# Whole-array matmuls issued as four column tiles, whole key tiles for VectorE, and later kernel loads in a gated attention and convolution kernel

## The chip, the cores and the metric

The kernel runs on one core of a Trainium2 chip. The metric is the device time of one execution in microseconds (us). The core has five engines that run side by side and each in program order: TensorE (PE; its weight loads are listed as PEld), VectorE (DVE), ScalarE (ACT), GpSimd (POOL) and SyncE (SP, which here only issues DMAs).

## The reference

The input x has 2048 tokens of 640 features. Two branches are mixed by a gate g = sigmoid(x . gate_w):

```
k_shift = causal 4-tap convolution of A_k by A_shift_k, per feature;  kv = k_shift * A_v
a = x * (causal long convolution of kv by A_ssm_k over 2048 tokens, by FFT + kv * A_ssm_D)
q = x @ wq (32 heads of 20);  k = x @ wk;  v = x @ wv   (one key and value head for all)
b = softmax(q k^T / sqrt(20)) v, heads joined, @ wo
out = g * a + (1 - g) * b
```

## The kernel before, in words

**Work.** The attention scores are 32 groups G, each of four heads and 512 queries (8 groups for each of four query blocks). A group has 16 key tiles j of 128 keys. So there are 32 x 16 x 4 = 2048 score tiles (G, j, r) of 128 keys by 512 queries, r being the head within the group. A head has 20 features, with a bound on the score in row 20, so the score matmul (`score`, L1462) uses a 32-row strip of the array, at row 32 r, and four heads can run side by side. The product with the values (`PVmm`, L1542) uses a 32-column strip, four heads side by side again, and adds up over the 16 key tiles in PSUM bank 6.

**Who takes the exponential.** Most tiles go to ACT. They are cut into units of alternately three and two tiles (`stream`); PSUM banks 0 to 2 hold a three-tile unit and banks 3 and 4 a two-tile one. ACT writes their exponentials to ETA (1536 elements per partition) or ETB (1024), L1499. The other tiles go to DVE, without an exponential: for each (G, j) listed in `DVE_J`, two of the four heads are left out of the units; DVE turns each score tile into 16-bit integers (L1526, PSUM to the scratch PS in ES), and then makes four versions of it with four shifts (`dexp`, L1535), each 1024 elements because it covers both heads. Four products with differently weighted values (vneg) add up to the exponential. `DEXP` holds all of this. Groups 0, 1 and 31 have no DVE tiles.

**The rest.** The convolutions are matmuls too: L1802 (four taps as diagonal matrices), L1883 to L1893 (the spectra of kv and of the long kernel, with tables of cosines in TE and TO), the product of spectra on POOL (L1912), and L1937 (back to time). Query projections (L1353) and output projections (L1970, L1675, at the end L1705) complete them. These use the whole 128 by 128 array, and their results leave PSUM banks 5 and 7 (for projections of the output 6 as well) through DVE. The score tiles for DVE use banks 5 and 7 also.

**Order.** A scheduler in the kernel (`Scheduler`) walks through modelled time and writes a fixed order for each engine. PE's main queue has the score units and the value products; in the gaps before the next unit's bank comes free it places other work (`pick_work`), and dummy matmuls on a zero tile (L2031, the filler) when PE's busy share over a window falls below `FILL`. A charge `SWITCH` stands for a change between the row-strip, column-strip and whole-array forms; the forms are named by `MODE`. The order of the first 400 operations is set by a table of priorities `PRO`.

**Loads.** Query rows of block 0 reach the tile qT0 by way of DRAM: the projections are stored to scr_q, read back (`q_ld`, qT<-scr_q), and four further DMAs bring the row with the bound (`crow`, qT<-cr). The long kernel is loaded in five parts by transposing DMAs (kst<-in_A_ssm_k_dram, L1815, in `ssm_rows`) and stored to scr_k (scr_k<-kst). All of these are issued by SP.

Of the kernel before, what the change touches and what calls it, by code (L numbers as in the profile page):

```python
# [25 lines left out]
SLA = 0.5  # L26
SLB = 0.5
SLACK = 0.05
SLACK0 = 0.8
FILL = 0.7  # L30
# [3 lines left out]
MODE = {"qk": "r", "dqk": "r", "pv": "c", "fillc": "c", "q2": "m"}  # L34
SWITCH = 0.096
PATIENCE = 2.0
ROOM = 0.3
OLD = 6.0
YOUNG = 4.0
WAITN = 0.5  # L40
EAGER = 0.5
# [4 lines left out]
IDLE = 0.3  # L46
# [3 lines left out]
NE = 8  # L50
PACE0, PACE1 = 0.12, 0.85
NAB = 7
NPS = 2
NXK = 2
NEX = 2
# [124 lines left out]
class Scheduler:  # L180
# [189 lines left out]

    def head(self, t):
# [10 lines left out]
    def pick_work(self, t):  # L382
# [5 lines left out]
        self.gap = 0.0  # L388
        if self.float_left:
            f = self.float_left.pop(0)  # L390
            return f
        if self.rows and not (m is not None and m.cont):
            best = None
            for gr in self.gcand:
                if gr.rides and gr.ready <= t and (gr.mms[0].row not in self.rows or t - gr.ready >= EAGER):
# [52 lines left out]
        sw = SWITCH if self.mode != "f" else 0.0  # L448
        self.gap = gap if m is not None else 0.0
        if self.open is not None:  # L450
            gr = self.open
            mm = gr.mms[gr.pos]
            if mm.ready <= t and mm.cost + sw <= gap + slack and (sw == 0.0 or gap + slack - sw >= ROOM):
                return mm
            return None
        if self.mode != "f" and self.main_started and gap + slack - sw < ROOM:
# [3 lines left out]
        for gr in self.gcand:  # L460
            if gr.rides and t - gr.ready < PATIENCE:
# [139 lines left out]
    def emit(self, nc):  # L601
# [66 lines left out]
        for cm in reversed(cms):  # L668
# [23 lines left out]
PORTW = 0.2  # L692
# [6 lines left out]
PRO = {-36: 30.289, -35: 13.475, -32: -1999.683, -31: -10.662, -30: -10.829, -29: -699.986, -27: -999.665, -25: 37.435, -24: -994.513, -23: -10.798, -22: -10.591, -21: -1999.67, -20: -994.615, -19: -699.723, -16: 9.092, -15: -9.029, -14: -1199.944, -13: 5.095, -12: 20.143, -9: 5.099, -8: 13.254, -7: -994.804, -6: -9.289, -4: -699.504, -3: -4999.742, -2: -10.682, 1: 0.616, 4: 2.987, 5: 15.039, 6: -9.203, 11: 0.76, 16: 9.26, 24: 19.987, 25: -994.685, 27: 15.337, 30: -0.692, 31: 30.005, 37: 30.215, 52: 5.365, 54: -0.868, 55: 30.071, 57: 5.231, 58: 15.455, 59: -2990.013, 64: 9.055, 70: -1199.81, 76: -2999.664, 82: -3.929, 83: 3.034, 87: -2999.536, 105: -4999.602, 107: -1999.746, 109: 13.118, 111: 13.407, 114: -3.558, 122: 30.238, 124: -999.836, 127: -4999.976, 131: -994.809, 132: -1199.778, 139: -994.917, 140: -999.979, 143: 5.147, 144: 15.321, 158: -699.827, 160: 0.745, 162: 30.257, 163: -699.856, 165: -6.569, 167: 0.643, 177: -4999.827, 182: -1199.714, 185: -1199.995, 187: -699.756, 195: 0.855, 196: -994.815, 198: -994.895, 201: 20.124, 203: 30.414, 207: -10.894, 208: 15.19, 210: -1999.911, 211: -10.819, 216: -1999.841, 221: -10.967, 226: -4999.61, 227: -699.623, 237: -1199.573, 238: 20.138, 242: -699.816, 243: 15.307, 246: -4.013, 247: -1199.8, 249: -9.35, 252: 3.435, 260: -10.868, 262: 3.241, 266: -9.336, 269: -10.687, 272: -4999.664, 276: 20.344, 278: -0.864, 279: -0.634, 282: 9.372, 286: 15.447, 288: 13.048, 295: 0.76, 298: -4999.657, 300: -994.682, 305: -3000.0, 309: -10.635, 311: -699.78, 315: -10.683, 318: 15.346, 325: 9.458}  # L699
# [7 lines left out]
DVE_J = ((), (), (1, 4, 8, 13, 14), (1, 4, 9, 14), (1, 5, 8, 12, 14), (2, 3, 5, 8, 11, 14),  # L707
# [1383 lines left out]
```

## Time and profile before

| | before |
|---|---|
| median of 3 runs | 829.33 us (828.38 to 832.37) |
| profiled execution | 829.54 us |
| its span, first to last instruction | 827.7 us |
| mean granted TensorE clock | 0.993 of full speed |
| PE, ACT, DVE, POOL busy | 97%, 97%, 81%, 45% |

The span leaves out about 1.8 us around the instructions. A busy share counts an instruction from its start to its modelled or recorded end, so two that overlap in a pipeline make an engine look busier than the rate of its work. Starts of successive instructions give the rate.

### The profile page before, as it was taken

To read this page: it belongs to the slowest core of one execution; us is meant where nothing else is said; L and a number is where in the kernel's file an instruction comes from. 1 tells how busy PE (TensorE), PEld (TensorE's weight loads), DVE (VectorE), ACT (ScalarE), POOL (GpSimd) and SP (SyncE) were. 2 spreads that over 40 slices of the span, in tenths; PEclk is the share of its full clock that TensorE was granted. 3 is DMA by queue.
4 is the path that set the end of the run, shared out by engine and by line. 5 is a ranking of instruction groups with operands and counts; after the bars stand their busy time and mean duration, and the time that the engine had idled before them with its cause. 6 is when DMAs were issued, how large, how long until landed. Compare 5 with 4: busy or idle time off the path is not lost.

```text
span 827.7 us, 19391 instructions
## 1 busy us (share of the span) xinstructions
PE 801.7 (97%) x8153; PEld 308.4 (37%) x8172; DVE 666.3 (81%) x1356; ACT 803.8 (97%) x716; POOL 370.2 (45%) x370
## 2 busy tenths in 40 slices
PE   7999999999999999999999999999999999999997
PEld 4344433333323433333333333433334432243334
DVE  6853797899988787888888899888898889778655
ACT  5999999999999999999999999999999999999996
POOL 3412000366562556666246676556667664400000
PEclk8999999999999999999999999999999999999999
DMA  5968312100030000110002210000100000131211
GB/s 170 223 140 181 90 53 58 26 26 21 28 90 23 20 9 21 53 34 21 17 18 56 60 47 21 15 17 12 46 23 21 15 14 3 56 76 39 85 47 34
DMA packets 65704, 41.60 MB, mean 50 GB/s; under 512 B 43379, under 2 KB 60496, under 8 KB 65616
## 3 DMA queue, kind: packets, MB, share of 16 engines
q1 hardware_dynamic: 65040, 40.14, 17.9%
q8 instruction: 64, 1.05, 0.5%
q10 hardware_dynamic: 576, 0.22, 0.1%
q14 instruction: 24, 0.20, 0.1%
HBM read 22.93 MB, written 11.13 MB: 41 GB/s over the span
## 4 chain that ended last, share of the span: by engine, by line
ACT 50%; PE 46%; DVE 1%; DMA 1%; SPq 0%; issue 0%
ACT ETA L1499 30%; ACT ETB L1499 20%; PE ps L1462 15%; PE ps L1542 12%; PE ps L1893 5%; PE ps L1937 4%; PE ps L1802 2%; PE ps L2031 2%; PE ps L1970 1%; PE ps L1890 1%; PE ps L1353 1%; DMA xn<-in_A_q_dram 1%; SPq L793 0%; PE ps L1187 0%; PE ps L1675 0%
## 5 line engine op out<-in xcount | busy, mean ns | idle before, releaser
L1499 ACT ACTIVATE ETA<-ps 128x1536 bf16<-128x1536 f32 (+1 forms) x349 | 529.2, 1516 | 4.0 <-PE ps L1462 3.5
L1499 ACT ACTIVATE ETB<-ps 128x1024 bf16<-128x1024 f32 x348 | 380.4, 1093 | 2.9 <-PE ps L1462 1.7
L1462 PE MATMUL ps<-qT,kT 32*128 32x512 bf16 (+2 forms) x2176 | 315.3, 371 | 13.5 <-ACT ETA L1499 3.6
L1535 DVE TENSOR_SCALAR ES<-ES 128x1024 int16<-128x1024 int16 x612 | 263.5, 486 | 19.6 <-PE ps L1542 16.4
L1526 DVE TENSOR_SCALAR ES<-ps 128x512 int16<-128x512 f32 x306 | 209.2, 685 | 60.0 <-PE ps L1462 58.5
L1912 POOL TENSOR_TENSOR Pp<-X,K 128x512 f32<-128x512 bf16 x120 | 140.9, 1185 | 76.2 <-DVE ES L1535 48.5
L1462 PEld LDWEIGHTS ps<-qT,kT 32*128 32x128 bf16 x2176 | 77.5, 91 | 220.2 <-ACT ETA L1499 88.1
L1542 PE MATMUL ps<-ETA,vaug 128*32 128x512 bf16 (+2 forms) x1124 | 153.0, 370 | 0.0
L1542 PE MATMUL ps<-ETB,vaug 128*32 128x512 bf16 (+2 forms) x746 | 144.1, 370 | 0.1
L1542 PE MATMUL ps<-ES,vneg 128*32 128x512 bf16 x1224 | 126.2, 380 | 0.0
L1638 POOL TENSOR_TENSOR oTn<-acc,rbc 128x512 bf16<-128x512 f32 x24 | 31.8, 1326 | 117.4 <-DVE ES L1535 86.8
L1912 POOL TENSOR_TENSOR Y<-Pp 128x256 f32<-128x256 f32 x80 | 58.2, 727 | 49.9 <-DVE ES L1535 43.2
L1912 POOL TENSOR_TENSOR Pp<-Pp 128x512 f32<-128x512 f32 x40 | 51.0, 1275 | 37.2 <-DVE ES L1535 31.7
L2031 PE MATMUL ps<-TE,zeros 128*32 128x512 bf16 x732 | 62.8, 384 | 0.2
L1912 POOL TENSOR_TENSOR AB<-Y 128x512 bf16<-128x512 f32 x40 | 50.9, 1281 | 24.5 <-DVE ES L1535 21.4
L1542 PEld LDWEIGHTS ps<-ES,vneg 128*32 128x32 bf16 x1224 | 40.3, 96 | 31.5 <-issue 4.2
L1638 POOL TENSOR_TENSOR oT<-acc,rbc 128x512 bf16<-128x512 f32 x7 | 9.0, 1287 | 85.2 <-DMA rbc<-scr_d 39.4
L1542 PEld LDWEIGHTS ps<-ETA,vaug 128*32 128x32 bf16 x1124 | 31.6, 94 | 37.2 <-issue 35.1
L1542 PEld LDWEIGHTS ps<-ETB,vaug 128*32 128x32 bf16 x746 | 30.0, 94 | 27.9 <-issue 26.0
L1898 DVE COPY EX<-ps 128x512 f32<-128x512 f32 x40 | 27.4, 684 | 8.6 <-PE ps L1893 8.1
L1901 DVE TENSOR_TENSOR K<-ps,EX 128x512 bf16<-128x512 f32 x40 | 27.5, 687 | 6.3 <-PE ps L1893 5.9
L1901 DVE TENSOR_TENSOR X<-ps,EX 128x512 bf16<-128x512 f32 x40 | 27.4, 684 | 1.7 <-PE ps L1893 1.2
(181 smaller groups left out, 692.6 us busy)
## 6 DMA issues: line engine op xcount, KB each, us to landing
rbc<-scr_d SPq DMA_DIRECT2D x31, 256.0 KB
scr_o<-oTn SPq DMA_DIRECT2D x24, 128.0 KB, 1.7
kv<-in_A_v_dram SPq DMA_DIRECT2D x4, 640.0 KB
scr_k<-kst SPq DMA_DIRECT2D x5, 512.0 KB, 6.4
ssm_kT<-scr_k SPq DMA_DIRECT2D x10, 256.0 KB, 3.8
out_dram<-outsb SPq DMA_DIRECT2D x15, 160.0 KB, 2.0
xn<-in_A_q_dram SPq DMA_DIRECT2D x3, 640.0 KB
scr_q<-xT SPq DMA_DIRECT2D x15, 128.0 KB, 1.7
```

Of the source, the lines that this page charges most:

```text
L1462: return e.matmul(self.bank(bk, n, n * t), T["kT0" if first(G, jt) else "kT4"][32 * r:32 * r + 32, 128 * jt:128 * jt + 128], T[k][32 * r:3 ...
L1499: x = op("act", lambda e: e.activation(et(n)[:, 0:w], self.ps[:, lo:lo + w], ACT.Exp, scale=OCT, bias=-K0 * OCT), [("ps", base[n % 2] + k) ...
L1526: self.evac(gr, "dve", lambda e, bk, c=c: e.tensor_scalar(P[:, c], self.bank(bk), FINE, FTOP, ALU.mult, ALU.add), (), [kP], c_dve(512))
L1535: V(lambda e, E=E, t=t: e.tensor_scalar(E, P, 1.0 / FINE, SHIFT[t] - FTOP / FINE, ALU.mult, ALU.add), [kP], [("ES", z)], C4X, port=True, n ...
L1542: return op("pe", lambda e: e.matmul(self.bank(b, n)[32 * r:32 * r + 32, :], v[:, j, :], src, start=(j == 0 or cut and j == 4 * EARLY), st ...
L1638: self.pool(lambda e: e.tensor_tensor(out, T["acc"][:, :], T["rbc"][:, :], ALU.mult), ["acc", "rbc"], [key], 1.27, prio=p, port=True, name ...
L1893: self.mm(gr, lambda e, bk, lhs=lhs, rhs=rhs, comp=comp, st=(comp, mc) == (0, 0), sp=(comp, mc) == (1, NG - 1): e.matmul(self.bank(bk, 256 ...
L1898: self.evac(gr, "dve", lambda e, bk, EX=EX: e.tensor_copy(EX[:, :], self.bank(bk)), (), [("EX", ex)], c_dve(512))
L1901: self.evac(gr, "dve", lambda e, bk, EX=EX, Z=Z, h=h, alu=alu: e.tensor_tensor(Z[:, h].rearrange("p i a c -> p a i c"), parts(self.bank(bk ...
L1912: f = lambda e: e.tensor_tensor(out, a, b, alu)
L1937: self.mm(gr, lambda e, bk, lhs=lhs, fc=fc, comp=comp, par=par, z=z: e.matmul(self.bank(bk, 256, 256 * par), lhs, W[:, z, par, :, comp, :] ...
L2031: sch.filler, *sch.filler2 = ([[lambda e, r=r, st=st, b=b, n=n: e.matmul(self.bank(b, n)[32 * r:32 * r + 32, :], self.T["zeros"][:, 0:32], ...
```

## The change

**Column tiles.** A helper `mm4` issues a whole-array matmul as four, each with 32 of the 128 weight columns and the same moving data, at column positions 0, 32, 64 and 96. It replaces the whole-array matmul in the taps, the spectra, the inverse, the query projections of `qtiles` and the output projections of the main stretch. The last projections (`tail_mm`) and the work before the main stretch keep the old form. `MODE` puts these groups in the same form as the value products, and the scheduler charges `SWITCH` only where the form changes.

**Whole key tiles.** A (G, j) in `DVE_J` now gives all four heads to DVE. The table has 83 entries instead of 153, so DVE takes 332 tiles instead of 306 and ACT 1716 instead of 1742. `dexp` makes versions of 2048 elements. PS has one buffer instead of two, ES five slots of 2048 instead of eight of 1024, the spectra one EX buffer instead of two and six AB buffers instead of seven.

**Loads.** The third to fifth part of the long kernel wait until the last `crow` DMA of query block 0 has landed. The scheduler's figures for `q_ld` and `crow` are larger.

**Numbers of the scheduler.** Slacks, patience, the `FILL` share, and the tables `PRO` and `DVE_J` are new.

```diff
-SLA = 0.5
-SLB = 0.5
+SLA = 0.4
+SLB = 0.3
...
-FILL = 0.7
+FILL = 0.6
...
-MODE = {"qk": "r", "dqk": "r", "pv": "c", "fillc": "c", "q2": "m"}
+MODE = {"qk": "r", "dqk": "r", "pv": "c", "fillc": "c", "q2": "m", "kc": "c", "spec": "c", "inv": "c", "op": "c", "op1": "c",
+        "qpc": "c"}
...
-NE = 8
+NE = 5
...
-NAB = 7
-NPS = 2
+NAB = 6
+NPS = 1
...
-NEX = 2
+NEX = 1
...
-DVE_J = ((), (), (1, 4, 8, 13, 14), (1, 4, 9, 14), (1, 5, 8, 12, 14), (2, 3, 5, 8, 11, 14),
+DVE_J = ((), (), (3, 7, 11), (3, 5, 11, 14), (2, 8, 9), (6, 12), (2, 8, 13), (6, 9, 12),
...
-C4X = 0.36
+C4X = 0.63
...
+    def mm4(self, e, out, lhs, rhs, **k):
+        for q in range(0, 128, 32):
+            x = e.matmul(out[q:q + 32], lhs[:, q:q + 32], rhs, tile_position=(0, q), **k)
+        return x
...
-        sb("ES", [128, NE + NPS, 1024], BF16)
+        sb("ES", [128, NE + NPS, 2048], BF16)
...
                 if G <= LASTG and j in DVE_J[G]:
-                    mine, rest = order[:2], order[2:]
-                    self.on_dve[G, j] = tuple(sorted(rest))
-                    order = rest + mine
+                    self.on_dve[G, j] = order
+                    continue
...
-                        self.mm(gr, lambda e, bk, ii=ii, j=j, t0=t0, c=c: e.matmul(
-                            self.bank(bk, 128, 128 * ii), T["kTr"][:, c, t0:t0 + 509:4], T["kdiag"][:, c, j, :],
+                        self.mm(gr, lambda e, bk, ii=ii, j=j, t0=t0, c=c: self.mm4(e, self.bank(bk, 128, 128 * ii), T["kTr"][:, c, t0:t0 + 509:4], T["kdiag"][:, c, j, :],
                             start=(j == 0), stop=(j == 3)), [("kTr", q), ("kTr", q - 1), "kdiag"], c_mm(128))
...
-                           after=self.crow0 + [self.g.writer["kvl", NB - 1]])
+                           after=self.crow0 + [self.g.writer["kvl", NB - 1]] + ([self.g.writer["qT0", 7, 4]] if c > 1 else []))
```

How the rows move is seen at three places. The first is SP early in the program, from the third store of query projections on. The kernel before has there:

```order
L793 DMA rbc<-scr_d 128x1x512
L793 DMA scr_k<-kst_55 128x16x128
L793 DMA scr_k<-kst_56 128x16x128
L1815 DMA_TRANSPOSE kst_55<-in_A_ssm_k_dram 128x16x128
L793 DMA scr_o<-oTn 128x512
L793 DMA scr_q<-qT 128x512
L1815 DMA_TRANSPOSE kst_56<-in_A_ssm_k_dram 128x16x128
L793 DMA qT<-scr_q 20x6x512 x4
L793 DMA qT<-cr 1x6x512 x4
L793 DMA scr_k<-kst_55 128x16x128
```

and the changed kernel, at the query rows of block 0:

```order
L800 DMA scr_q<-qT 128x512 x2
L1822 DMA_TRANSPOSE kst_55<-in_A_ssm_k_dram 128x16x128
L800 DMA den<-acc 128x1x16
L800 DMA qT<-scr_q 20x6x512 x4
L800 DMA qT<-cr 1x6x512 x2
L800 DMA scr_d<-rcp 128x16
L800 DMA qT<-cr 1x6x512 x2
L800 DMA scr_k<-kst_55 128x16x128
L1822 DMA_TRANSPOSE kst_56<-in_A_ssm_k_dram 128x16x128
L800 DMA rbc<-scr_d 128x1x512
```

The query rows now stand behind one transposing load instead of four, and right behind the first group's `den`.

The second place is PE in the stage of the spectra (ES,vneg are the DVE tiles' value products, ETA,vaug and ETB,vaug those of ACT's tiles). The kernel before:

```order
L1542 MATMUL ps<-ES,vneg 32x512 x2
L1542 MATMUL ps<-ETA,vaug 32x512
L1462 MATMUL ps<-qT,kT 128x512 x2
L1893 MATMUL ps<-ssm_kT,TE 128x256 x6
L1462 MATMUL ps<-qT,kT 128x512 x3
L1883 MATMUL ps<-Drow,TE 128x128
L1890 MATMUL ps<-ssm_kT,TE 128x128 x8
L1462 MATMUL ps<-qT,kT 128x512 x3
```

and the changed kernel, in the same stage:

```order
L1473 MATMUL ps<-qT,kT 128x512 x2
L1552 MATMUL ps<-ES,vneg 32x512 x4
L824 MATMUL ps<-ssm_kT,TE 32x256 x4
L1552 MATMUL ps<-ES,vneg 32x512 x4
L824 MATMUL ps<-ssm_kT,TE 32x256 x12
L1552 MATMUL ps<-ES,vneg 32x512 x4
L1473 MATMUL ps<-qT,kT 128x512 x3
L824 MATMUL ps<-Drow,TE 32x128 x4
L1552 MATMUL ps<-ES,vneg 32x512 x4
```

A whole-array row has become four column rows, and value products stand between them. Over the whole order PE has 13519 rows instead of 8174, and from the first score on 1329 changes of form instead of 1541 and 88 fillers (of four matmuls) instead of 183.

The third place is DVE among the first DVE tiles. The kernel before:

```order
L1526 TENSOR_SCALAR ES<-ps 128x512
L1837 TENSOR_SCALAR xn<-xn,gf 128x640
L1535 TENSOR_SCALAR ES<-ES 128x1024 x4
L1526 TENSOR_SCALAR ES<-ps 128x512
L1806 TENSOR_TENSOR kv<-ps,kv 128x4x128
```

and the changed kernel:

```order
L1545 TENSOR_SCALAR ES<-ES 128x2048 x3
L1536 TENSOR_SCALAR ES<-ps 128x512 x4
L1545 TENSOR_SCALAR ES<-ES 128x2048 x3
L1813 TENSOR_TENSOR kv<-ps,kv 128x4x128
L1545 TENSOR_SCALAR ES<-ES 128x2048
```

Two evictions and four versions of 1024 have become four evictions and four versions of 2048. ACT's rows are 343 of three tiles, 343 of two and one of a single tile, instead of 348, 348 and one of two.

## Rows read from the trace of the kernel before

**Rows 1.** The page: busy times, and the chain that ended last.

```profile
PE 801.7 (97%) x8153; PEld 308.4 (37%) x8172; DVE 666.3 (81%) x1356; ACT 803.8 (97%) x716; POOL 370.2 (45%) x370
...
ACT 50%; PE 46%; DVE 1%; DMA 1%; SPq 0%; issue 0%
```

**Rows 2.** Timeline of ACT (start, duration in us, engine, line, operation), undisturbed.

```profile
641.69 1.46 ACT L1499 ACTIVATE ETA<-ps 128x1536 bf16<-128x1536 f32 x1
643.02 1.04 ACT L1499 ACTIVATE ETB<-ps 128x1024 bf16<-128x1024 f32 x1
...
650.62 1.57 ACT L1499 ACTIVATE ETA<-ps 128x1536 bf16<-128x1536 f32 x1
```

**Rows 3.** Timeline of ACT, the first and the last exponential.

```profile
21.08 1.45 ACT L1499 ACTIVATE ETA<-ps 128x1536 bf16<-128x1536 f32 x1 [0.35 <-PE ps L1462]
...
819.22 1.23 ACT L1499 ACTIVATE ETA<-ps 128x1024 bf16<-128x1024 f32 x1
```

**Rows 4.** Groups by line and form: count, busy us, mean ns, idle before.

```profile
L1499 ACT ACTIVATE ETB<-ps 128x1024 bf16<-128x1024 f32 x348 | 380.4, 1093 | 2.9 <-PE ps L1462 1.7 <-PE ps L1542 0.6
...
L1535 DVE TENSOR_SCALAR ES<-ES 128x1024 int16<-128x1024 int16 x612 | 263.5, 486 | 19.6 <-PE ps L1542 16.4
L1526 DVE TENSOR_SCALAR ES<-ps 128x512 int16<-128x512 f32 x306 | 209.2, 685 | 60.0 <-PE ps L1462 58.5
...
L1066 DVE TENSOR_SCALAR TO<-TO 128x512 bf16<-128x512 bf16 x1 | 0.3, 283 | 0.0
```

**Rows 5.** Timeline of ACT around the first query rows.

```profile
78.11 1.48 ACT L1499 ACTIVATE ETA<-ps 128x1536 bf16<-128x1536 f32 x1
80.86 1.02 ACT L1499 ACTIVATE ETB<-ps 128x1024 bf16<-128x1024 f32 x1 [1.26 <-PE ps L1462]
...
84.97 1.45 ACT L1499 ACTIVATE ETA<-ps 128x1536 bf16<-128x1536 f32 x1 [0.82 <-PE ps L1462]
...
89.92 1.46 ACT L1499 ACTIVATE ETA<-ps 128x1536 bf16<-128x1536 f32 x1
```

**Rows 6.** Timeline of SP (DMA issues) and of PE there.

```profile
71.04 2.87 SPq L1815 DMA_TRANSPOSE kst<-in_A_ssm_k_dram  x1
74.10 1.54 SPq L793 DMA_DIRECT2D qT<-scr_q  x4
75.69 2.90 SPq L793 DMA_DIRECT2D qT<-cr  x4
...
80.41 0.39 PE L1462 MATMUL ps<-qT,kT 32*128 32x512 bf16 x2 [1.32 <-DMA qT<-cr]
```

**Rows 7.** Windows: length, busy us of each engine, then PE's granted clock.

```profile
84.00:86.00 2.00, 2.00 (x17) 1.08 (x15) 0.42 (x1) 1.18 (x2) 0.00 (x0) 0.50 0.95 204
```

**Rows 8.** Timeline of PE in the middle: row, column and whole-array forms.

```profile
400.18 0.39 PE L1462 MATMUL ps<-qT,kT 32*128 32x512 bf16 x4
400.50 0.40 PE L2031 MATMUL ps<-TE,zeros 128*32 128x512 bf16 x4
400.73 0.60 PE L1542 MATMUL ps<-ES,vneg 128*32 128x512 bf16 x8
401.27 0.60 PE L1462 MATMUL ps<-qT,kT 32*128 32x512 bf16 x3
```

**Rows 9.** Who PE's weight loads waited for: us in total, times, longest.

```profile
PEld ps L1462 <- ACT ETA L1499: 88.1, 265, 1.2
...
PEld ps L1462 <- ACT ETB L1499: 80.5, 220, 0.9
```

**Rows 10.** Timeline of PE: whole-array taps of 128 columns, then the scores.

```profile
60.60 1.09 PE L1802 MATMUL ps<-kdiag,kTr 128*128 128x128 bf16 x16
61.62 0.39 PE L1462 MATMUL ps<-qT,kT 32*128 32x512 bf16 x3
```

**Rows 11.** Timeline of PE in the last group: column tiles of 128.

```profile
810.10 0.24 PE L1542 MATMUL ps<-ETA,vaug 128*32 128x128 bf16 x3
810.11 0.23 PE L1542 MATMUL ps<-ETB,vaug 128*32 128x128 bf16 x1
...
810.28 0.23 PE L1542 MATMUL ps<-ETA,vaug 128*32 128x128 bf16 x3
```

**Rows 12.** One line: its DVE versions, minimum, median, maximum ns.

```profile
L1535 DVE TENSOR_SCALAR ES<-ES x612: 359/420/1504, 87.9 to 792.5; 128x1024 int16<-128x1024 int16 x153
```

**Rows 13.** Windows: all of the stretch with DVE tiles, and its fullest part.

```profile
80.00:790.00 710.00, 696.85 (x6901) 256.55 (x6913) 599.09 (x1194) 704.27 (x621) 344.37 (x320) 1.00 0.13 37
400.00:500.00 100.00, 98.67 (x996) 35.86 (x994) 90.13 (x178) 99.60 (x88) 50.04 (x49) 1.00 0.14 40
```

More of the change, by code (lines that the diff above doesn't have):

```diff
@@ L45 @@
 NPRO = 400
-IDLE = 0.3
+IDLE = 0.6
 WAITP = 4.0
@@ L369, in startable, with sw_of @@
         return True
+    def sw_of(self, gr):
+        return 0.0 if self.mode == MODE.get(gr.name, "f") else SWITCH
     def head(self, t):
@@ L388, in pick_work @@
         self.gap = 0.0
+        hungry = self.t["dve"] - t + sum(o.cost for o in self.cand["dve"] if o.ready <= t + LEAD) < LEAD
         if self.float_left:
@@ L394, in pick_work @@
             for gr in self.gcand:
-                if gr.rides and gr.ready <= t and (gr.mms[0].row not in self.rows or t - gr.ready >= EAGER):
+                if gr.rides and gr.ready <= t and (gr.mms[0].row not in self.rows or t - gr.ready >= (HURRY1 if hungry else EAGER)):
                     b = self.bank_for(gr, t)
@@ L460, in pick_work @@
         for gr in self.gcand:
-            if gr.rides and t - gr.ready < PATIENCE:
+            if gr.rides and t - gr.ready < (HURRY2 if hungry else PATIENCE):
+                continue
+            sw = self.sw_of(gr)
+            if sw and self.main_started and gap + slack - sw < ROOM:
                 continue
@@ L1568, in PV @@
                 for jd in DVE_J[G]:
-                    ra, rb = self.on_dve[G, jd]
+                    rows = self.on_dve[G, jd]
                     for u, z in enumerate(DEXP(G, jd)):
                         fl = []
-                        for t in range(m):
-                            for h, r in enumerate((ra, rb)):
-                                fl.append(PVmm(r, m * jd + t, T["ES"][:, z, 512 * h + w * t:512 * h + w * t + w], ("ES", z), late=u,
-                                               b=b, n=w, cost=0.216 / m if h else 0.003, after=[o]))
+                        for r in rows:
+                            fl.append(PVmm(r, jd, T["ES"][:, z, 512 * r:512 * r + 512], ("ES", z), late=u,
+                                           b=b, n=w, cost=0.003 if r < 3 else 0.216, after=[o]))
                         a = fl[0]
                         a.floating = True
-                        a.cols = frozenset((ra, rb))
+                        a.cols = frozenset(rows)
                         a.tail = tuple(fl[1:])
@@ L1936, in inverse @@
                     lhs, tk = self.table("TO" if par else "TI", comp, fc, 128 * q)
-                    self.mm(gr, lambda e, bk, lhs=lhs, fc=fc, comp=comp, par=par, z=z: e.matmul(
-                        self.bank(bk, 256, 256 * par), lhs, W[:, z, par, :, comp, :], start=(fc == 0 and comp == 0),
+                    self.mm(gr, lambda e, bk, lhs=lhs, fc=fc, comp=comp, par=par, z=z: self.mm4(e, self.bank(bk, 256, 256 * par), lhs, W[:, z, par, :, comp, :], start=(fc == 0 and comp == 0),
                         stop=(fc == NG - 1 and comp == 1)), [tk, ("AB", z, par)], c_mm(256))
```

77 lines of the change are left out of this document (37 added, 40 removed), and 11 rows, old and new, of the table DVE_J.

## The prediction

> **What bounds the kernel now.** I read the page first. PE and ACT are both busy 97% of the span, DVE 81%, and the chain that ended last is half ACT, half PE [rows 1]. Two engines at 97% can't both be the bound, so I went to the timeline of ACT. Undisturbed, a three-tile exponential starts 1.33 us before the next and a two-tile one 0.90 us: four pairs take 650.62 - 641.69 = 8.93 us, 2.233 a pair [rows 2]. The recorded 1.46 and 1.04 us overlap the next instruction, which is why ACT looks fuller than its rate. From the first exponential at 21.08 to the last at 819.22 are 798.1 us [rows 3], with 348 pairs between, as the count of two-tile ones has it [rows 4]. 348 x 2.233 = 777.1. So ACT runs at its own rate for all but 21.0 us of its stretch. Before it lie 21.1 us of start, behind it 7.3 us of end, and 1.8 us lie outside the span.
>
> PE is the other half of the chain because it is late now and then, not because it has no room. Its weight loads for the score units waited 88.1 + 80.5 us for ACT to free a bank [rows 9]. One sum over the whole order says the same: sets of matmuls that run side by side at 0.215 us for 512 columns and 0.06 us for 128 (below) give 598 us, and 1541 changes of form at 0.105 us give 162 more, 760 of 798. That leaves PE about 5% free, little enough to be late in places.
>
> Where do the 21.0 us go? One place is plain. Between 78.11 and 89.92 ACT does four pairs, 8.93 us of work, in 11.81 [rows 5]: 2.9 us lost. The cause is in SP's timeline: the reads of the query rows are issued from 74.10 and their `crow` DMAs until 78.6, behind a transposing load at 71.04, and PE's next score waited 1.32 us for qT<-cr until 80.41 [rows 6]. It cost more than that wait. [...] The other 18 us are scattered.
>
> **The change part by part.** The sum is made against the profiled execution, 829.5 us, which is the median (829.3) as far as can be told.
>
> *ACT's tiles.* DVE takes 332 instead of 306, ACT has 343 pairs instead of 348 and at the end one tile instead of two. Five pairs are 5 x 2.233 = 11.2 us. A lone tile is about 0.45 us shorter (1.33 - 0.90 = 0.43 a tile in rows 2). Together -11.6 us, and this term is on the path for as long as ACT is the bound.
>
> *Query rows.* In the new order of SP only one transposing load stands ahead of these reads instead of four, and they come right behind the first group's `den`. A group has 64 tiles, 64 x 2.233 / 5 = 28.6 us of ACT, so the first ends near 50 us and the third, which needs the rows, begins near 79. From their issue to PE's start they took 6.3 us (74.10 to 80.41), so they can land some 20 us before they are needed. I take the whole 2.9 us; the bounds are 0 and 2.9. The third long-kernel load now waits on SP for the last `crow`. Behind it stand stores to scr_k and scr_o and the next `den`, none of which feeds a score of this block, so I cost it at nothing. If the cover were gone, a late `den` would hold the accumulator, not ACT, for some 2 us.
>
> *Column form.* A set of four column matmuls of 128 takes 0.06 us: four such sets start at 810.10 to 810.28 [rows 11]. Sixteen whole-array taps of the same width take (1.09 - 0.23) / 15 = 0.057 us each [rows 10]. So the four cost what the one cost, and the weight loads of a set hide as they do now. A change of form costs (401.27 - 400.73) - 2 x 0.215 = 0.11, and 400.50 - 400.18 - 0.215 = 0.105 us, from row to column as from column to row [rows 8]; between filler and value products, both column, 400.73 - 400.50 = 0.23 there is next to none. The taps to the scores give the same 0.10 [rows 10]. So 212 changes fewer are 22 us of PE. The 95 fillers fewer are 20 us. Sets of value products fall from 832 to 793 as they stand in the order (four DVE tiles fill a set, two did not always), 8 us. Together PE's 760 become about 710 of 784: 9% free instead of 5%.
>
> [...]
>
> *What PE's room is worth.* Only the scattered 18 us can answer to it. Bounds: nothing, since a score unit behind a run of value products at a group's end is late whatever the filler was; and half, 9 us, as PE's free share about doubles. I take 3 us, nearer to nothing, because the scheduler's slack for other work ahead of a unit (`SLA`, `SLB`) changes as well and no row shows the new order's gaps.
>
> *DVE.* Evictions: 332 x 0.685 = 227 us against 209 [rows 4]. The versions: 1024 elements have a median of 0.420 us [rows 12], 512 in 16 bits took 0.283 [rows 4], so 1024 more are 2 x 0.137 = 0.27 and the median is 0.69. The mean of before lies 0.066 above its median, since some last up to 1.5 us [rows 12]. With the same excess a version takes 0.76 us, with twice the excess 0.82, and at twice the mean of before 0.97. At 0.76 they are 252 us against 264. DVE's whole load from 80 to 790 was 599 us of 710 [rows 13], 126 of it other work, and becomes 126 + 227 + 252 = 605 of about 695: 87% instead of 84%. The fullest 100 us now are at 90% and run at ACT's rate [rows 13]. So I cost DVE at nothing, with the margin below. POOL has 344 of 710 us and its waits are not ACT's. Fewer buffers (PS, EX, ES, AB) put the same work closer in order; DVE runs evictions and versions in turn anyway, and I cost them at nothing, with that same margin.
>
> *Start.* The order before the first exponential is new. No row prices it: 0, with 1 us either way.
>
> Sum: 829.5 - 11.6 - 2.9 - 3 = 812.0 us, which stands for the median too. With the bounds: 829.5 - 11.6 = 818 without either relief, 806 with all of it, and 1 us for the start: 805 to 819.
>
> **The rivals.**
>
> 1. *PE's room is given back.* The new order uses it up, or the 5300 more matmuls arrive late in the taps, where 1280 matmuls with their loads replace 320 (no row shows a late one). Then the scattered waits stay or grow by up to 8 us and the query rows alone count: 815 to 825. For it: PE had 5% free and was late all the same.
>
> 2. *DVE becomes the bound, and the kernel is slower.* Four evictions and four long versions stand in one row on DVE, and the next tiles' scores can't leave PSUM meanwhile. If DVE can't be filled beyond 90% (its best 100 us), the stretch takes (353 + 332 v) / 0.9 us for a version of v us. At v = 0.82 that is 695, ACT's own time; above v = 0.86 it is over today's 710 and the change loses; at the upper bound of 0.97 it is 750, and the kernel takes about 870. Against it: the median slope of 0.27 us for 1024 elements and half as many instructions that can be held up.
>
> 3. *The column form costs more.* If a set of 128 columns took twice the whole-array matmul, 660 x 0.057 = 38 us, PE would be at 748 of 784, 95% as now, and the relief gone: 815. [...] Rows 11 speak against it.
>
> 4. *The tile count does not tell.* If PE, not ACT, set the pace throughout, five pairs fewer would give nothing and the saved PE work everything: 829.5 - 50 = 780. Rows 2 and 9 speak against it.
>
> **How the numbers follow.** Chances: the forecast 0.70 (805 to 819), rival 1 0.15, rival 2 0.08, rival 3 0.04, rival 4 or anything else below 805 0.03. The time is 812. The range 803 to 823 leaves out rival 2, the far third of rival 1 and half of the last: under 0.2. About 0.5%, 4 us, is what a measurement of this kernel can tell from no change. Faster by more than that (below 825): 0.88; within it 0.05; slower 0.07, nearly all of rival 2.
>
> **What would show it.** ACT: 343 pairs, still 2.23 us each undisturbed, first to last exponential about 780 us, so that 14 to 15 us are lost instead of 21. Right for the query rows: no wait on qT<-cr near 79 us, no clock at 0.50 behind it. Column form: taps of 128 columns in sets of 0.057 to 0.06 us; PE's filler 88 sets. DVE: versions with a median near 0.69 and a mean near 0.76, DVE busy near 670 us. The prediction is wrong if the mean version is above 0.82 us and ACT waits for scores at group ends, if the gaps of ACT sum to more than 25 us, or if the first exponential comes later than 23 us.

## The result and the profile after

| | before | after |
|---|---|---|
| median of the first comparison | 829.19 us (828.38 to 832.37) | 817.95 us (812.48 to 820.07) |
| beside the first group of experiments | 828.15 us | 819.43 us (813.11 to 822.64) |
| profiled execution, its span | 829.54, 827.7 us | 812.48, 810.7 us |
| PE, ACT, DVE, POOL busy | 97%, 97%, 81%, 45% | 95%, 98%, 82%, 47% |

The kernel is faster: the ratio is 0.9846 (95% interval 0.9804 to 0.9887), and 0.9885 (0.986 to 0.991) in the second comparison. Its executions spread more than those of before beside them (825.75 to 830.02 us in the second comparison): ten lie between 812.48 and 822.64 us, median 818.9. The profiled one is the fastest of them, so the decomposition below is that of a good execution, and a second profile, at 822.64 us, is read beside it.

The page after has these busy times, chain and costly groups, which answer to [rows 1, 4]:

```profile
PE 770.7 (95%) x13513; PEld 317.9 (39%) x13517; DVE 663.1 (82%) x1102; ACT 790.6 (98%) x706; POOL 380.4 (47%) x370
...
ACT 61%; PE 34%; DVE 4%; issue 1%; DMA 0%; DVEq 0%
...
L1510 ACT ACTIVATE ETB<-ps 128x1024 bf16<-128x1024 f32 x343 | 379.6, 1107 | 0.0
...
L1536 DVE TENSOR_SCALAR ES<-ps 128x512 int16<-128x512 f32 x332 | 221.7, 686 | 69.9 <-PE ps L1473 66.5
L1545 DVE TENSOR_SCALAR ES<-ES 128x2048 int16<-128x2048 int16 x332 | 236.8, 768 | 4.7 <-PE ps L1552 2.5
```

PE carries 31 us less and is no longer half of the chain; ACT has 343 two-tile exponentials instead of 348. The timeline of ACT has its first and last exponential, which answer to [rows 3], and the two largest gaps between:

```profile
15.62 1.45 ACT L1510 ACTIVATE ETA<-ps 128x1536 bf16<-128x1536 f32 x1 [0.26 <-PE ps L1473]
...
61.51 1.45 ACT L1510 ACTIVATE ETA<-ps 128x1536 bf16<-128x1536 f32 x1 [2.11 <-PE ps L1473]
...
274.69 1.45 ACT L1510 ACTIVATE ETA<-ps 128x1536 bf16<-128x1536 f32 x1 [2.26 <-PE ps L824]
...
803.25 0.63 ACT L1510 ACTIVATE ETA<-ps 128x512 bf16<-128x512 f32 x1
```

The span is 827.7 - 810.7 = 17.0 us shorter, in three pieces. The first exponential comes 21.08 - 15.62 = 5.5 us earlier. From first to last are 787.6 us instead of 798.1, 10.5 less, where five pairs are 11.2. Behind the last, 7.45 us instead of 8.48. So ACT loses as much between its exponentials as before, 787.6 - 343 x 2.233 = 21.7 us against 21.0.

The largest single loss, 2.6 us at 274.69, is the end of a group. DVE's and PE's timelines:

```profile
271.34 2.54 DVE L1545 TENSOR_SCALAR ES<-ES 128x2048 int16<-128x2048 int16 x4
...
273.99 0.39 PE L1552 MATMUL ps<-ES,vneg 128*32 128x512 bf16 x4
274.21 0.39 PE L1552 MATMUL ps<-ETA,vaug 128*32 128x512 bf16 x3
```

DVE works on the four versions of the group's last whole key tile until 273.88, and on PE the value products that read ETA stand behind the last of them. ACT goes on when these are under way. All six profiles of this order have this loss (2.6 us, 3.2 in whole-array form, where ACT's row names the value products); none of the order before has one above 1 us behind 100 us.

PE's timeline shows one loss that the kernel before did not have (taps are kdiag,kTr; four column matmuls make one set):

```profile
57.79 0.98 PE L824 MATMUL ps<-kdiag,kTr 128*32 128x128 bf16 x55
60.73 0.36 PE L824 MATMUL ps<-kdiag,kTr 128*32 128x128 bf16 x9 [1.96 <-issue]
...
67.98 0.38 PE L1552 MATMUL ps<-ETA,vaug 128*32 128x512 bf16 x1 [0.79 <-issue]
```

Fifty-five is no multiple of four: PE stops within a set, where the moving data and the bank are those of the matmul before, and the row names no releaser. The next score, and with it the exponential at 61.51, comes that much later. In the kernel before, no such wait after 25 us is longer than 0.3 us.

### The profile page after: what moved, and what is told of

It reads as the page before. It is cut to its first block, busy times and chain, and to the rows that moved or that the text cites. A ratio compares the mean times of both kernels' runs of the same rounds, so it can differ in the third digit from the quotient of the medians.

```text
span 810.7 us, 29855 instructions
## 1 busy us (share of the span) xinstructions
PE 770.7 (95%) x13513; PEld 317.9 (39%) x13517; DVE 663.1 (82%) x1102; ACT 790.6 (98%) x706; POOL 380.4 (47%) x370
## 3 DMA queue, kind: packets, MB, share of 16 engines
q8 instruction: 105, 1.72, 0.9%
## 4 chain that ended last, share of the span: by engine, by line
ACT 61%; PE 34%; DVE 4%; issue 1%; DMA 0%; DVEq 0%
ACT ETA L1510 37%; ACT ETB L1510 24%; PE ps L1473 12%; PE ps L824 10%; PE ps L1552 9%; DVE ES L1536 1%; PE ps L2033 1%; PE ps L1199 0%; DVE ES L1545 0%; DMA xn<-in_A_q_dram 0%; PE ps L1085 0%; PE ps L1713 0%; PE ps L1380 0%; DVE X L1905 0%; DVE EX L1902 0%
## 5 line engine op out<-in xcount | busy, mean ns | idle before, releaser
L1510 ACT ACTIVATE ETA<-ps 128x1536 bf16<-128x1536 f32 x344 | 524.4, 1525 | 8.6 <-PE ps L1473 5.3
L1473 PE MATMUL ps<-qT,kT 32*128 32x512 bf16 (+2 forms) x2176 | 331.8, 371 | 27.4 <-ACT ETA L1510 13.1
L1536 DVE TENSOR_SCALAR ES<-ps 128x512 int16<-128x512 f32 x332 | 221.7, 686 | 69.9 <-PE ps L1473 66.5
L1545 DVE TENSOR_SCALAR ES<-ES 128x2048 int16<-128x2048 int16 x332 | 236.8, 768 | 4.7 <-PE ps L1552 2.5
L1552 PE MATMUL ps<-ETA,vaug 128*32 128x512 bf16 (+2 forms) x1106 | 134.4, 369 | 0.8 <-issue 0.8
L1552 PE MATMUL ps<-ETB,vaug 128*32 128x512 bf16 (+2 forms) x738 | 133.1, 369 | 0.0
L1552 PE MATMUL ps<-ES,vneg 128*32 128x512 bf16 x1328 | 117.6, 383 | 0.0
L824 PE MATMUL ps<-ssm_kT,TE 128*32 128x128 bf16 (+1 forms) x1280 | 40.1, 247 | 0.1
L824 PE MATMUL ps<-ssm_kT,TO 128*32 128x128 bf16 (+1 forms) x1280 | 38.3, 247 | 0.4 <-DVE ES L1536 0.4
L2033 PE MATMUL ps<-TE,zeros 128*32 128x512 bf16 x352 | 30.7, 386 | 0.8 <-DVE acc L1630 0.8
```

Source lines behind the costliest of these rows:

```text
L824: x = e.matmul(out[q:q + 32], lhs[:, q:q + 32], rhs, tile_position=(0, q), **k)
L1473: return e.matmul(self.bank(bk, n, n * t), T["kT0" if first(G, jt) else "kT4"][32 * r:32 * r + 32, 128 * jt:128 * jt + 128], T[k][32 * r:3 ...
L1510: x = op("act", lambda e: e.activation(et(n)[:, 0:w], self.ps[:, lo:lo + w], ACT.Exp, scale=OCT, bias=-K0 * OCT), [("ps", base[n % 2] + k) ...
L1536: self.evac(gr, "dve", lambda e, bk, c=c: e.tensor_scalar(P[:, c], self.bank(bk), FINE, FTOP, ALU.mult, ALU.add), (), [kP[r]], c_dve(512))
L1545: V(lambda e, E=E, t=t: e.tensor_scalar(E, P, 1.0 / FINE, SHIFT[t] - FTOP / FINE, ALU.mult, ALU.add), kP, [("ES", z)], C4X, port=True, nam ...
L1552: return op("pe", lambda e: e.matmul(self.bank(b, n)[32 * r:32 * r + 32, :], v[:, j, :], src, start=(j == 0 or cut and j == 4 * EARLY), st ...
```

## The experiments

"Lost" in this section is the sum, over successive exponentials on ACT's timeline, of the distance between their starts less 1.333 us after three tiles and 0.90 after two. Nine of the twelve kernels keep, on every engine, the order of the kernel that they were made from, but for the entries named; three were planned anew by the scheduler (the last of experiment 3 and the two of experiment 5).

**1. The changed kernel again, and with whole taps.** The edit of the second:

```diff
-                        self.mm(gr, lambda e, bk, ii=ii, j=j, t0=t0, c=c: self.mm4(e, self.bank(bk, 128, 128 * ii), T["kTr"][:, c, t0:t0 + 509:4], T["kdiag"][:, c, j, :],
+                        self.mm(gr, lambda e, bk, ii=ii, j=j, t0=t0, c=c: e.matmul(self.bank(bk, 128, 128 * ii), T["kTr"][:, c, t0:t0 + 509:4], T["kdiag"][:, c, j, :],
```

> The changed kernel once more, to see what its executions have in common. The first profile had a span of 810.7 us with the first exponential at 15.62 us and a granted clock of 1.00 from the beginning; three other executions had 815 to 818 us and a mean clock of 0.992 to 0.994. Theory: those differ at the start alone (a lower granted clock in the first 10 us, first exponential at 18 to 21 us), and the stretch from the first to the last exponential is 787 to 789 us in each; median 813 to 819. Rival: the difference lies in the main stretch (late instructions in the taps, other clock stages), and the stretch varies by 4 us or more.

> The changed kernel in the same order, with the 320 tap matmuls alone issued whole-array (960 matmuls fewer near 30 to 75 us, 18 more changes of form, 1.9 us). Theory (the two waits of 1.96 and 0.79 us in the middle of tap sets are late instructions): these waits vanish, ScalarE's gaps at 61.5 and 69.5 us (2.23 and 1.09 us of loss) go, and the time is 2 to 3.5 us below that of the changed kernel. Rival: the waits come from something that the taps need (the moving data or the DMA traffic at 54 to 64 us): they stay in place, and the time is the same or up to 2 us longer.

> The changed kernel with the taps alone whole-array, once more, beside the run with its start set back, and to see whether it stays below the changed kernel. Theory: 810 to 815 us, granted clock 0.997 or more in most executions, first exponential at 15.6 us. Rival: the first run was lucky with the clock; then 816 to 820 us, as the changed kernel has.

Measured: the changed kernel 819.43 us (ratio 0.9885); with whole taps 812.46 (0.9822, 0.9796 to 0.9848) and again 814.60 (0.9842, 0.9808 to 0.9877). Ten executions of the one have a median of 818.9, twelve of the other 813.2: by the medians the taps' column form costs 5.7 us, by the ratios 3.6 to 5.2, more than the 2 to 3.5 expected.

The first theory on the spread fell. In the second profile of the changed kernel, with a span of 820.8 us, the first exponential is at 15.78 us: the start is not what varies. That profile's PE timeline, and windows of 2 us there (busy PE, PEld, DVE, ACT, POOL, then PE's granted clock, the DMA engines' busy share and GB/s; packets count where they start, so a share can exceed 1):

```profile
55.80 1.09 PE L824 MATMUL ps<-kdiag,kTr 128*32 128x128 bf16 x64
56.82 0.39 PE L1473 MATMUL ps<-qT,kT 32*128 32x512 bf16 x3
...
60.90 0.36 PE L824 MATMUL ps<-kdiag,kTr 128*32 128x128 bf16 x9 [1.85 <-issue]
```

```profile
58.00:60.00 2.00, 1.04 (x57) 0.82 (x55) 0.69 (x1) 1.70 (x2) 0.00 (x0) 1.00 1.37 85
60.00:62.00 2.00, 1.10 (x28) 0.69 (x32) 0.00 (x0) 0.24 (x1) 0.00 (x0) 0.84 0.93 205
62.00:64.00 2.00, 1.64 (x42) 0.74 (x31) 0.60 (x1) 1.85 (x2) 0.00 (x0) 0.50 0.46 121
...
68.00:70.00 2.00, 2.00 (x45) 0.92 (x37) 1.97 (x4) 0.84 (x1) 1.10 (x1) 0.50 1.04 213
70.00:72.00 2.00, 2.00 (x46) 0.95 (x42) 1.71 (x2) 1.63 (x2) 0.55 (x1) 0.60 0.83 197
```

The pause is at the same matmul as in the first profile. There the clock stayed at 1.00; here, with PE busy 1.04 and 1.10 of 2 us, it fell to 0.50 of full speed until about 71.6, and ACT loses 9.6 us before 100 us instead of 5.8. Another late matmul (0.94 us at 84.91) follows. ACT loses 6.3 us more than in the first profile behind 100 us too, most of it where the clock was at 0.50 again for 3.4 us each, from 212, 710 and 737 us, with no late instruction; so the taps are not the whole of the spread. With whole taps neither profile has a wait for issue above 0.3 us; ACT loses 3.1 us before 100 us in the first. In the second the clock fell all the same: PE waited for DVE (0.72 and 0.56 us at 84.17 and 86.69), then the clock was 0.50 from 88 to 94, and 7.5 us were lost before 100 us. So a pause for late instructions is one thing that stood ahead of a fall of the clock, not the only one.

That PE waits for instructions there can be read from the traces. The pages list a queue of instruction packets (packets, MB, share of the DMA engines), here before the change, after it, and with whole taps:

```profile
q8 instruction: 64, 1.05, 0.5%
...
q8 instruction: 105, 1.72, 0.9%
...
q8 instruction: 98, 1.61, 0.9%
```

The three traces hold 16355, 27067 and 25151 instructions of PE and its weight loads, some 256 to a packet. Four profiles have pauses of this kind above 0.5 us, six in all. In each of them a packet of this queue starts 2.2 to 2.5 us before PE goes on, and lands 1.2 to 1.5 us before; at the first pause it starts at 58.52 and lands at 59.48, and PE goes on at 60.73. The six also stand at one place in the count: 1725 and 1981 instructions come before the end of the two in the first profile, 1729 and 2753 in the second, 2753 and 1725 in the two of experiments 2 and 5, and these differ by multiples of 256 to within four. Taps in column form use up 256 instructions, 128 matmuls with their loads, in 2 x 1.02 = 2.04 us, less than those 2.2 to 2.5; whole ones take 8.2 us for as many (estimates from the rows above and [rows 10]).

The first two rows of the timeline above answer to [rows 10]: 64 column taps take as long as 16 whole ones took, 1.02 us to the next score. Here the form cost PE's array nothing; it cost instructions, 64 matmuls for 16.

**2. The column form alone, in both orders.** The changed kernel with whole-array matmuls in the same order:

```diff
     def mm4(self, e, out, lhs, rhs, **k):
-        for q in range(0, 128, 32):
-            x = e.matmul(out[q:q + 32], lhs[:, q:q + 32], rhs, tile_position=(0, q), **k)
-        return x
+        return e.matmul(out, lhs, rhs, **k)
```

and the kernel before, in its own order, with `mm4` at the same eight places (the second time at all but the taps), of which one is:

```diff
-                    self.mm(gr, lambda e, bk, lhs=lhs, rhs=rhs, comp=comp, st=(comp, mc) == (0, 0), sp=(comp, mc) == (1, NG - 1): e.matmul(
-                        self.bank(bk, 256, 256 * comp), lhs, rhs, start=st, stop=sp), [tk] + rk, c_mm(256))
+                    self.mm(gr, lambda e, bk, lhs=lhs, rhs=rhs, comp=comp, st=(comp, mc) == (0, 0), sp=(comp, mc) == (1, NG - 1): self.mm4(e, self.bank(bk, 256, 256 * comp), lhs, rhs, start=st, stop=sp), [tk] + rk, c_mm(256))
```

> The changed kernel with every instruction in its place, but each set of four column tiles issued as one whole-array matmul again: about 5600 matmuls fewer, 276 more changes of form (at 0.105 us some 29 us more work for TensorE), same tiles on ScalarE and VectorE. Theory (the gain is ScalarE's 26 tiles fewer; the column form is cheap and its relief is hardly used): 0 to 8 us slower than the changed kernel, so 815 to 825 us, and no late instructions in the taps. Rival A (TensorE's room is what brings the gain): back to the time of the kernel before, 827 us or more, with the waits spread over the whole stretch. Rival B (the column form itself costs): 3 us or more faster than the changed kernel, 812 us or less.

> The kernel before with its order, tables and tiles, but with the same matmuls issued as four column tiles: 172 changes of form fewer (18 us of TensorE's time), 5600 matmuls more. Theory: within 0.5% of the kernel before, 825 to 833 us, since ScalarE has as many tiles as before and the scattered waits hang on VectorE, on group ends and on the fixed order. Rival A (room on TensorE is time): 820 us or less. Rival B (more instructions arrive late): 834 us or more, with waits for issue inside the tap matmuls.

> The kernel before in its own order, with the matmuls of spectra, inverse and projections issued as column tiles but the taps whole. The run with all of them as column tiles lost 7.9 us of ScalarE's time before 100 us (4.2 in the kernel before) and 14.7 after it (16.8). Theory: the first is the taps' late instructions, the second the room that fewer changes of form give; without the first the time is 1 to 3 us below the kernel before (825 to 827 us where that has 828), with no wait for issue above 0.5 us. Rival A: the room is worth nothing and the 2 us after 100 us were chance: within 0.5 us of the kernel before. Rival B: spectra and projections as column tiles come late too: waits for issue after 100 us, 830 us or more.

Measured: whole form in the new order 833.00 us, ratio 1.0071 (1.0045 to 1.0098), slower than before. Column form in the old order 828.16 us, 1.0009 (0.9995 to 1.0023); without the taps 827.86, 1.0000 (0.9972 to 1.0028).

Here my theory of a cheap form whose relief is hardly used failed, and rival A won, in the new order only. There the form is worth 833.0 - 819.4 = 13.6 us, and 20 against the version with whole taps. The chain of the whole-form run, and windows of the main stretch, first of that run, then of the changed kernel:

```profile
PE 60%; ACT 32%; DVE 6%; DMA 1%; issue 1%; DVEq 0%
```

```profile
80.00:773.00 693.00, 668.51 (x6394) 246.25 (x6394) 570.45 (x901) 673.90 (x590) 351.74 (x316) 1.00 0.12 34
```

```profile
80.00:773.00 693.00, 666.04 (x11410) 265.42 (x11398) 587.41 (x929) 687.77 (x608) 352.78 (x317) 1.00 0.12 35
```

PE is as busy, but ACT comes through 590 instructions in that time instead of 608. Lost: 40.8 us, 36.7 of them after 100 us, and spread: 67 gaps of 0.2 to 1 us take 26.8 of them, where the version with whole taps has 27 such gaps and 9.6 us. In the order are 276 changes of form more, 29 us at 0.105 [rows 8]. My reading, which no run shows by itself: the new order sets other work right behind value products and ahead of scores with the smaller slacks (`SLA`, `SLB`, `SLACK0`), and with two changes of form around it that work no longer fits its gap.

In the old order, planned with room for those changes, taking them away gives ACT 1.6 us of 21.1 (19.5 lost without the taps), and the median does not move: rival A of that run held, not the 1 to 3 us that I expected. With the taps too, one late instruction (1.18 us at 79.66) fell just ahead of the wait for the query rows, and 7.9 us were lost before 100 us instead of 4.2, 14.7 after it instead of 16.8.

**3. The start.** On SP, the second half of the first block of x stands behind wq and the second block in the kernel before, right behind the first half in the changed one. Three kernels: the kernel before with these entries exchanged after scheduling (the diff: operation 0 is the first half, 1 the second, 2 wq, 3 the second block); the changed kernel with whole taps and `behind(self.g.all[1], self.g.all[3])`; and the kernel before with the number of operation 1 in `PRO` at -996.8 instead of 0.616, which does the same but plans all the rest anew.

```diff
         sch.run()
+        sp, lin = sch.order["sp"], sch.linear
+        def behind(o, p):
+            for q in (sp, lin):
+                q.remove(o)
+                q.insert(q.index(p) + 1, o)
+        for i in (3, 2):
+            behind(self.g.all[i], self.g.all[1])
```

> The kernel before, in its own order on every engine, with two entries of SP's queue exchanged: the second half of the first block of x comes ahead of wq and of the second block. Nothing is planned anew, unlike in the run that changed a number of the table. Theory: the wait of 3.39 us before the second ten transposes goes, the first exponential comes 2 to 3.5 us earlier (17.5 to 19 us instead of 21.1), and the time is 2 to 3.5 us below the kernel before, 824.5 to 826 us. Rival: the second block of x then lands later and the transposes at 11 us wait for it; first exponential within 0.7 us of 21.1, time the same.

> The changed kernel with whole taps, in the same order on every engine, but on SP the second half of the first block of x is issued behind wq and the second block again, as in the kernel before. Theory (the earlier start is this load order): TensorE's second ten transposes wait some 3 us again, the first exponential comes at 18.5 to 20.5 us instead of 15.6, nothing gives it back later, and the time is 3 to 5 us above the run with whole taps. Rival: the earlier start comes from the order of TensorE's and VectorE's own work; then the first exponential stays below 17 us and the time is less than 1.5 us longer.

> The kernel before with one number of its table of priorities changed, so that SP issues the second half of the first query block's x right behind the first half, ahead of wq and of the other blocks, as the changed kernel does. The scheduler plans the rest anew, with as many tiles on every engine. Theory (the changed kernel's earlier start is this order of loads): TensorE's second ten transposes no longer wait 3.39 us, the first exponential comes at 15.5 to 17.5 us instead of 21.1, and the time is 3 to 5.5 us below the kernel before, 823 to 825 us. Rival: what follows is due at the same times anyway (keys, taps, query rows), so a wait behind the start takes the gain back: 827 us or more.

Measured: exchanged, 824.76 us, ratio 0.9962 (0.9947 to 0.9977); set back, 821.60, 0.9921 (0.9892 to 0.995), 7.0 above the run with whole taps beside it; planned anew, 833.41, 1.0054 (1.0033 to 1.0076). PE's transposes of x that need the second half, on its timeline in the kernel before, then exchanged, then set back:

```profile
8.29 1.26 PE L1187 MATMUL ps<-ident,xn 128*128 128x128 bf16 x10 [3.39 <-DMA xn<-in_A_q_dram]
```

```profile
3.92 2.46 PE L1187 MATMUL ps<-ident,xn 128*128 128x128 bf16 x20 [0.24 <-DMA xn<-in_A_q_dram]
```

```profile
8.67 2.33 PE L1199 MATMUL ps<-ident,xn 128*128 128x128 bf16 x20 [4.99 <-DMA xn<-in_A_q_dram]
```

The first exponential is at 16.64 us when exchanged (21.08 before) and at 20.98 when set back (16.07). Nothing behind it gives it back: 798.4 us from first to last in the exchanged run, 798.1 before. But 21.08 is a late start even for the old order of loads: four profiles with it have 20.05, 20.80, 20.98 and 21.08, so the exchange is worth 3.4 to 4.4 us at the first exponential. So two entries of one queue are worth 3.1 us in the median on the old kernel, and up to 7 on the new one. There the two profiles lie 9.2 us apart: 4.9 at the first exponential, and 4.2 in what ACT loses. From 95 to 115 us alone 5.8 more are lost, with the clock at 0.50 from 92 to 112 us, longer than in the run beside it (88 to 94). With six executions each, spread over 8 and 10 us, the 7.0 is rough. The replanned run had its start 3.1 us earlier and lost more than that in a new order (2.4 us more between the exponentials and 3.2 behind the last): a number of a tuned table can't be changed alone.

**4. The query rows.** The kernel before, its order kept, with the transposing load at 71.04 [rows 6] moved behind the eight DMAs of the query rows:

```diff
         sch.run()
+        cr = sp[[o.name for o in sp].index("q_ld") + 7]
+        ld = [o for o in sp[:sp.index(cr)] if o.iss == 3.0][-1]
...
+        for q in (sp, lin):
+            q.remove(ld)
+            q.insert(q.index(cr) + 1, ld)
```

> The kernel before, in its own order on every engine, with one entry of SP's queue moved: the fourth transposing load of the long kernel comes behind the eight DMAs of the query rows instead of ahead of them. Theory (the term of 2.9 us): the query rows land some 3 us earlier, TensorE no longer waits for the row with the bound near 80 us, the clock stays at 1.00, ScalarE's losses of 1.42, 0.96 and 0.45 us go, and the time is 2 to 3 us below the kernel before, 825 to 826 us. Rival: the load that was moved is late instead (spectra wait for the long kernel) or the wait goes elsewhere: time within 0.7 us of the kernel before.

Measured: 827.44 us, ratio 0.9992 (0.9981 to 1.0002). SP's and PE's timelines:

```profile
71.72 1.49 SPq L793 DMA_DIRECT2D qT<-scr_q  x4
73.25 2.91 SPq L793 DMA_DIRECT2D qT<-cr  x4
76.20 2.10 SPq L1815 DMA_TRANSPOSE kst<-in_A_ssm_k_dram  x1
```

```profile
88.32 0.75 PE L1802 MATMUL ps<-kdiag,kTr 128*128 128x128 bf16 x10 [1.23 <-DVE ES L1526]
```

The wait near 80 us and the fall of the clock are gone, as the theory has it: four sets of filler that PE's timeline has from 84.52 us start 0.22 us apart, as they do at 1.00, where [rows 7] have 0.50. But at 88.32 PE waits 1.23 us for a DVE tile, and ACT at 89.49 with it. ACT loses 2.8 us before 100 us instead of 4.2, and the median shows 0.4 (the interval allows 1.6). The rival was right: most of it is taken by what is late next. The other half of this edit in the change, the wait put on the later loads, moves nothing: with it taken out, the scheduler writes the same rows, in the same order, for all five engines; SP only waits once less.

**5. Planned anew: whole form, and loads after the taps.** The changed kernel with `mm4` whole and `MODE` as before; and, in column form, with the second to fifth long-kernel load waiting for the last taps:

```diff
-MODE = {"qk": "r", "dqk": "r", "pv": "c", "fillc": "c", "q2": "m", "kc": "c", "spec": "c", "inv": "c", "op": "c", "op1": "c",
-        "qpc": "c"}
+MODE = {"qk": "r", "dqk": "r", "pv": "c", "fillc": "c", "q2": "m"}
...
-                           after=self.crow0 + [self.g.writer["kvl", NB - 1]] + ([self.g.writer["qT0", 7, 4]] if c > 1 else []))
+                           after=self.crow0 + [self.g.writer["kvl", NB - 1]] + ([self.g.writer["kv", NDC - 1, 15]] if c > 0 else []))
```

> The changed kernel with whole-array matmuls everywhere and MODE as before, so that the scheduler knows of every change of form and plans its order for it: whole key tiles, the load order and the scheduler's new numbers stay. Theory (tiles and start carry the gain, and the whole form lost 20 us in the other run only because the order was planned for the column form): 813 to 822 us. Rival (with four tiles fewer per group on ScalarE the rest of TensorE's work no longer fits without the column form): 826 us or more, with ScalarE's losses spread over the stretch, 30 us or more against 21.

> The changed kernel, taps as column tiles, but the second to fifth part of the long kernel are loaded only when the taps are done, so that few transfers run beside the taps; the scheduler plans the rest anew, and the spectra start later. Theory (instructions come late because their blocks travel on the same DMA engines as the transposing loads): no wait for issue above 0.5 us on TensorE between 50 and 90 us, clock 1.00 there, ScalarE's losses before 100 us near 3 us. Rival (column tiles of 128 elements are drawn faster than instructions arrive, whatever else is moved): waits for issue of 1 us or more stay inside the taps. The time itself, 808 to 825 us, decides nothing here.

Measured: 839.47 us (1.0132, 1.009 to 1.0175) and 850.38 (1.0248, 1.0203 to 1.0294). Both start at 15.7 to 15.9 us. ACT's timeline of the first:

```profile
645.83 1.45 ACT L1507 ACTIVATE ETA<-ps 128x1536 bf16<-128x1536 f32 x1 [6.06 <-PE ps L1549]
...
674.87 1.02 ACT L1507 ACTIVATE ETB<-ps 128x1024 bf16<-128x1024 f32 x1 [4.99 <-PE ps L1549]
...
705.65 1.45 ACT L1507 ACTIVATE ETA<-ps 128x1536 bf16<-128x1536 f32 x1 [7.01 <-PE ps L1549]
```

and DVE's and PE's timelines at the first of these:

```profile
640.98 1.52 DVE L1533 TENSOR_SCALAR ES<-ps 128x512 int16<-128x512 f32 x2
642.53 2.50 DVE L1542 TENSOR_SCALAR ES<-ES 128x2048 int16<-128x2048 int16 x4
```

```profile
645.19 0.40 PE L1549 MATMUL ps<-ES,vneg 128*32 128x512 bf16 x4
645.42 0.38 PE L1549 MATMUL ps<-ETA,vaug 128*32 128x512 bf16 x1
```

The group's last whole key tile is evicted until 642.5, its four versions last until 645, and only then can PE's value products end the group; it is these that ACT's row names. Within 4 us ahead of and 2 us behind the copies of the accumulator some 30 of ACT's 46 us are lost here, some 7 both before and after the change. The second kernel has such gaps in column form too (8.18 us at 165.53, 3.70 at 266.99). So neither time says what the form or the loads are worth. The 839 is outside the 813 to 822 that I expected and inside the rival's 826 or more, but the losses are not spread as the rival has them. It doesn't decide between the two: whether whole key tiles could be planned well without the column form stays open. On late instructions the second kernel speaks: with DMA's busy share at 0.25 instead of 1.37 between 58 and 60 us the wait is still there, shorter.

```profile
59.86 0.36 PE L824 MATMUL ps<-kdiag,kTr 128*32 128x128 bf16 x9 [1.14 <-issue]
```

So the rival holds: here the number of instructions made them late with few other transfers beside them. That other transfers make it worse is not shown. The packet was under way for 1.03 us here and 0.96 in the first profile, and PE went on 1.2 us after it landed in both; the wait is shorter because the packet started 1.1 us ahead of the pause instead of 0.25. Why it started earlier stays open.

## Why the prediction was right, and where it was not

The forecast of 812 us with 803 to 823 holds the 818 to 819 measured. Its sum did not come out as it was made; several terms were wrong in opposite directions. So the number owes something to luck: the start gave 3 to 7 us and was put at 0, the taps took 4 to 6 and were put at nothing. The number alone could not tell either, since 818 is the forecast's own bound without any relief and lies in rival 1's 815 to 825.

**ACT's tiles, -11.6: right.** 343 pairs at the same 2.23 us and one tile at the end: 10.5 + 1.0 us came off behind the first exponential in the first profile. Only the condition that came with it, "as long as ACT is the bound", hid more than the prediction said: in the whole-form run PE is 60% of the chain and the 11.6 us are gone.

**Start, 0 with 1 us either way: the step that failed most.** "No row prices it" was wrong. PE's timeline of before has the wait of 3.39 us for x, the new order of SP has the two halves side by side, and the exchange alone gives 4.4 us at the first exponential and 3.1 in the median.

**PE's freed room, -3: nothing of the kind.** I took it as a bonus on scattered waits. On the old order the form gives 0 (interval of 2.3 us either way); after the change ACT still loses 21.7 us, not 14 to 15. In the new order the kernel is slower than before without that room. I take it that the room is already spent there, on the work that the smaller slacks pack in; that is argued, not shown.

**Query rows, -2.9: right in place, too large.** No wait near 79 us, and from 78 to 90 us the clock was 1.00, where [rows 7] have 0.50. But the run with only that gave 0.4 us, at most 1.6 by its interval; the term supposed that nothing else was late within the same 10 us.

**Column form at no cost on the array: right.** Sets of 0.057 us, some 14 ns a matmul (64 column taps in 1.09 us at 55.80 in the second profile).

**Late instructions, rival 1 at 0.15: its mechanism happened.** It was named for the taps and found there: 5.7 us in the median, 3.3 in the first profile (2.23 and 1.09 us lost at 61.51 and 69.46). I should have counted it in, since the number of matmuls was known. The queue of instructions moved 105 packets of together 1.72 MB, 16 KB each; in the taps PE waits up to 1.96 us, and goes on 1.2 to 1.5 us after such a packet has landed.

**DVE at nothing, rival 2 at 0.08: right in sum.** Versions have a mean of 0.768 us (0.76 estimated), DVE is busy 663 us (670), and ACT loses some 7 us around the ends of groups as before. But one end of a group waits 2.6 us for its last whole key tile (274.69), the mechanism of rival 2 in small. And the prediction did not see how narrow this is: a change of plan alone makes group ends wait up to 8 us for that tile. **Rivals 3 and 4** did not happen: the array's time is the same (1.02 us for 64 column taps as for 16 whole ones), and ACT sets the pace (61% of the chain).

Put together from the runs, 828.2 - 11.6 - 3.1 (start) - 0.4 (rows) + 5.7 (taps) = 818.8, against 819.4. The agreement is better than the terms deserve, as the start was worth 7.0 by the other run. Shown by runs are the taps, the start, the rows and the form in both fixed orders; the whole key tiles were never run alone, so their term rests on the count and on ACT's rate.

The version with whole taps beats both kernels: 813.2 us over twelve executions.

## What to carry to other kernels

Cutting matmuls into column tiles cost the array nothing here (1.02 us for 64 column taps as for 16 whole ones), but it multiplies instructions: keep it where it saves changes of form next to other column work (0.105 us each in [rows 8]), and leave dense runs of short matmuls whole (the taps so gave 5.7 us). Price room on an engine in the order that will use it: taking work away from a fixed order gave nothing, taking it back from an order that had spent it cost 14 to 20 us. Compare the first few DMAs of two kernels entry by entry before calling a start unpriced, and test single edits of a tuned schedule with the order held fixed, because the three kernels that were planned anew came out 5 to 31 us slower than the ones they were made from, in large part by waits that the edit did not aim at.

## What was not expected of the hardware

- One and the same pause of PE had two outcomes: after 1.96 us in the first profile of the changed kernel the granted clock stayed at 1.00, after 1.85 us in the second it was 0.50 until about 71.6 us, and ACT lost 9.6 us before 100 us instead of 5.8. In the second run with whole taps it also fell with no late instruction, when PE was busy 1.44, 1.62 and 1.28 us of three successive stretches of 2 us (82 to 88 us).
- With 55 to 60 matmuls started in 2 us, and as many weight loads, PE waited for instructions 1 to 2 us; with 27 in 2 us, in the same place and with the same transfers beside it, never above 0.3 us. PE used up the 256 instructions of a packet in some 2.0 us of such taps, and a packet took 2.2 to 2.5 us from its start until PE went on.
